# Batch 0's transform of a Fourier-and-MLP kernel: the last sums of phase 0 given to TensorE, with a new order of the opening

## The chip, the cores and the metric

The kernel runs on one core of a Trainium2 chip. The metric is device microseconds for one execution, the median of several runs. The engines are TensorE (PE, whose weight loads are listed as PEld), VectorE (DVE), ScalarE (ACT), GpSimd (POOL) and SyncE (SP), whose queue issues all the DMAs. Each engine takes its own instructions strictly in the order in which they are written, and waits for the others by semaphores.

## The reference

```python
batch, seq, dim = (8, 3008, 256)
X = np.fft.fft(x, axis=1)
X = np.fft.fft(X, axis=2)
attn_out = X.real.astype(np.float32)
...
x = attn_out.reshape(B * S, D)
h = x @ w_in          # 256 -> 2048
r = np.maximum(h, 0.0)
g = s * (r * r) + b
return (g @ w_out).astype(np.float32)   # 2048 -> 256
```

So the real part of a two-dimensional Fourier transform, for each of eight batches, goes through a two-layer network with a squared ReLU.

## The kernel before, in words

The transform along the 256 features is folded into w_in: `fold_w_in` multiplies the decoded w_in by cosine and sine tables (`feat_sb`) in four parts of 512 columns, and the results, split into a high and a low part, are the weights `wd_h` and `wd_l` of the first layer. The transform along the sequence stays. It uses symmetry: sequence rows are summed and subtracted (`load_rows`, line 502, and `load_pairs`, line 507), then the two halves of the features are summed and subtracted (`load_halves`, lines 515 and 516, the last level of sums), which gives the tile `cs` in `folded[0]`: eight leaves of 96 rows for each of two phases. Four rows of tile each lie apart and are put in place by ScalarE (`gather`, line 479). `transform(su, ph)` then combines leaves (`leaves_x`, `leaves_y`) and multiplies them with the table `dft_sb`; its helper `pair` does so for two leaves, with four matmuls of 96 columns at line 561: the cosine table on the sums of the feature halves, the sine table on their differences. The results go through DVE (lines 569 and 570) and ScalarE into the blocks `spec_h` and `spec_l`, high and low part of the spectrum. Feature 128 (the Nyquist feature) has a path of its own, `nyquist`, with many small POOL instructions (lines 349 to 369) and the matmuls of line 449.

A batch has 3 blocks of 502 columns, a block 16 steps. A step of the first layer is six matmuls (line 641) of weights and spectrum in high and low parts; DVE (lines 647, 650, 651) and ScalarE (652, 667, 673) make the activation and its high part `gh`, POOL or DVE the low part `gl` (line 676). A step of the second layer is twelve matmuls (line 696); in block 0's first four steps it is four plain fp32 matmuls instead (line 686). Everything in PSUM passes through two rings of four banks, `ab` and `po`; a bank can be written again only when its readers are done.

The order of all work is written out by hand as letters: `START` for batch 0 with all loads, then `BATCH` seven times. Each letter advances one generator in the dictionary `work` by one piece: X loads an x tile, N the Nyquist rows, r a piece of w_in, R of w_out, t a table, c the feature tables; x, d, g (phase 0) and y, Y (phase 1) are the sums on tiles, k and K the gathers; a, b, e decode w_in (A, B, E w_out; the addition at line 301 is POOL's), w folds it; n, m are the Nyquist path, s and u the transform of batch 0, phases 0 and 1; L, D, G, S are first layer, activation, low part and second layer of a step. All engines get their instructions in this order, so a letter's place sets its place in five queues at once.

Of the kernel before, what the change touches and what calls it, by code (L numbers as in the profile page):

```python
# [15 lines left out]
P = 128  # L16
# [4 lines left out]
R = 96  # L21
# [95 lines left out]
def _dft_tables():  # L117
# [45 lines left out]
    return np.ascontiguousarray(out.astype(np.float32))  # L163


def _turn_table():

    t = np.arange(P)
    t[T:] = 0
    a = np.pi * (2 * t + 1) / Q  # L170
    b = np.pi * (2 * t + 1) / H
    c = np.pi / 4 - b
    v = np.stack([np.tan(a), np.tan(b), np.tan(c), np.cos(c) / np.cos(b)], axis=1)
    return np.ascontiguousarray(np.concatenate([v, -v], axis=1).astype(np.float32))


def _feature_tables():

    l = np.arange(D)[:, None]
    d = np.arange(P)[None, :]  # L180
    c, s = _unit(2 * l * d, D)
    c[:, 0] *= 0.5

    s[:, 0] = np.where(l[:, 0] % 2 == 0, -1.0, 1.0)
    t = np.concatenate([c, -s], axis=1).astype(np.float32)
    return np.ascontiguousarray(t.reshape(2, P, 2 * P))
# [52 lines left out]
def kernel(ctx: ExitStack, tc: tile.TileContext, xq, xn, dft, turn, feat, w_in, w_out, s, b, out):  # L239
# [26 lines left out]
    feat_sb = const.tile([P, 2, 2 * P], F32, name="feat_sb")  # L266
    sb_s = const.tile([P, 1], F32, name="sb_s")
    sb_b = const.tile([P, 1], F32, name="sb_b")
    turn_sb = const.tile([P, 8], F32, name="turn_sb")
# [48 lines left out]
    def fold_w_in(f):  # L318

        at = slice(f * 512, (f + 1) * 512)  # L320
        pool, name = ((ps_ab, "ab"), (ps_o, "po"))[f in FOLDS_IN_SUMS]
        ps = [pool.tile([P, 512], F32, name=name) for _ in range(2)]
        for c in range(2):
            for kind in range(2):
                nc.tensor.matmul(  # L325
                    ps[kind], feat_sb[:, c, kind * P:(kind + 1) * P], halves[f, c], start=c == 0, stop=c == 1
                )
            yield
        row = rows[f][0:1]
        nc.scalar.copy(row, ps[1][0:1])  # L330
        split(wd_h[:, 1, at], wd_l[:, 1, at], ps[1], nc.vector)
        yield
        split(wd_h[:, 0, at], wd_l[:, 0, at], ps[0], nc.vector)
        yield
        nc.sync.dma_start(wny_dram[:, at], row)
        yield
        nc.sync.dma_start(wny[:, 4 * f:4 * f + 4], wny_dram[0, at].rearrange("(j p) -> p j", p=P))
        yield
# [127 lines left out]

    spec_tiles = {}
# [39 lines left out]
    def load_pairs(tiles, ph):  # L507
        for t in tiles_in_turn(tiles):
            (sub if ph else add)(t[:, 1 + 2 * ph], t[:, 0], t[:, 2])
            yield  # L510

    def load_halves(tiles, ph):
        for c, t in enumerate(tiles_in_turn(tiles)):
            t, v = t[:, 1 + 2 * ph], folded[0][:, ph, c + 2]
            add(v[:, :P], t[:, :P], t[:, P:])
            sub(v[:, P:], t[:, :P], t[:, P:])
            yield
# [5 lines left out]
    def gathers(ph):  # L523
        for c in range(NX):
            gather(folded[0], c, slice(ph, ph + 1))
            yield
# [24 lines left out]
    def transform(su, ph):  # L551
# [191 lines left out]
    def load_constants():  # L743
        nc.sync.dma_start(feat_sb, feat.rearrange("c p d -> p c d"))
# [99 lines left out]
    def second():  # L844
# [10 lines left out]
        "x": load_rows(tiles), "d": load_pairs(tiles, 0), "g": load_halves(tiles, 0), "k": gathers(0),  # L855
        "y": load_pairs(tiles, 1), "Y": load_halves(tiles, 1), "K": gathers(1),
# [74 lines left out]
```

## Time and profile before

| | us |
|---|---|
| median of 3 runs | 1592.61 |
| lowest and highest | 1591.66, 1593.21 |
| the profiled execution | 1592.15 |
| its span on the core | 1590.4 |
| PE busy | 1559.5 (98%) |
| ACT busy | 1268.6 (80%) |
| DVE busy | 1251.7 (79%) |
| POOL busy | 916.6 (58%) |

The span is the profiled execution without what lies around it, 1.75 us here. Times in rows are microseconds from the span's start. An engine's busy time is the sum over its instructions; PE's is modelled, since matmuls are pipelined, so that a row of several matmuls runs a little into the next. What ended an idle time stands in a row behind an arrow; it costs something only where the engine is the one that all others wait for.

### The profile page before, as it was taken

To read this page: it belongs to the slowest core of one execution; us is meant where nothing else is said; L and a number is where in the kernel's file an instruction comes from. 1 tells how busy PE (TensorE), PEld (TensorE's weight loads), DVE (VectorE), ACT (ScalarE), POOL (GpSimd) and SP (SyncE) were. 2 spreads that over 40 slices of the span, in tenths; PEclk is the share of its full clock that TensorE was granted. 3 is DMA by queue.
4 is the path that set the end of the run, shared out by engine and by line. 5 is a ranking of instruction groups with operands and counts; after the bars stand their busy time and mean duration, and the time that the engine had idled before them with its cause. 6 is when DMAs were issued, how large, how long until landed. Compare 5 with 4: busy or idle time off the path is not lost.

```text
span 1590.4 us, 21860 instructions
## 1 busy us (share of the span) xinstructions
PE 1559.5 (98%) x7494; PEld 1367.2 (86%) x7494; DVE 1251.7 (79%) x1912; ACT 1268.6 (80%) x1361; POOL 916.6 (58%) x541
## 2 busy tenths in 40 slices
PE   5899999999999999999999999999999999999998
PEld 2488898888888889888888888888888888988887
DVE  5888788699877998779886898868888699775563
ACT  4789787887787878878777887878788787787886
POOL 5455565555665556655565656555556555675554
PEclk8999999999999999999999999999999999999999
DMA  6402101021010100111001100102101020010000
GB/s 243 125 15 86 33 1 59 1 86 34 1 60 27 60 33 1 60 53 34 33 14 46 66 21 33 60 1 78 38 4 60 0 86 33 1 33 30 4 27 26
DMA packets 26070, 67.84 MB, mean 43 GB/s; under 512 B 5220, under 2 KB 10724, under 8 KB 25960
## 3 DMA queue, kind: packets, MB, share of 16 engines
q1 hardware_dynamic: 25960, 66.44, 12.5%
q8 instruction: 60, 0.98, 0.3%
q14 instruction: 50, 0.41, 0.1%
HBM read 41.70 MB, written 24.73 MB: 42 GB/s over the span
## 4 chain that ended last, share of the span: by engine, by line
PE 94%; DVE 2%; ACT 0%; issue 0%; POOL 0%; ACTq 0%; DVEq 0%; POOLq 0%
PE po L696 60%; PE ab L641 30%; PE ab L561 3%; PE po L686 1%; DVE uv L347 0%; DVE even L647 0%; DVE h L650 0%; DVE h L651 0%; PE ab L325 0%; DVE gl L676 0%; POOL gl L676 0%; DVE x L569 0%; ACT h L667 0%; ACT h L652 0%; DVE wd_l L263 0%
## 5 line engine op out<-in xcount | busy, mean ns | idle before, releaser
L676 POOL TENSOR_TENSOR gl<-h,gh 128x1004 fp32r<-128x1004 f32 x373 | 808.0, 2168 | 589.4 <-ACT gh L673 433.6
L652 ACT ACTIVATE h<-h 128x1004 f32<-128x1004 f32 x384 | 398.8, 1039 | 256.5 <-DVE h L651 238.8
L647 DVE SCALAR_TENSOR_TENSOR even<-ebc,wny,ab 128x502 f32<-128x502 f32 x384 | 281.4, 733 | 218.4 <-PE ab L641 209.1
L696 PE MATMUL po<-gh,wo_h 128*128 128x502 f32 (+1 forms) x1520 | 448.6, 377 | 0.0
L696 PE MATMUL po<-gh,wo_l 128*128 128x502 f32 (+1 forms) x1520 | 445.9, 375 | 0.0
L667 ACT ACTIVATE h<-h 128x1004 f32<-128x1004 f32 x380 | 395.6, 1041 | 12.0
L673 ACT CAST gh<-h 128x1004 fp32r<-128x1004 f32 x380 | 391.2, 1029 | 12.1
L696 PE MATMUL po<-gl,wo_h 128*128 128x502 f32 (+1 forms) x1520 | 384.6, 376 | 0.6 <-POOL gl L676 0.6
L696 PEld LDWEIGHTS po<-gl,wo_h 128*128 128x128 f32 x1520 | 286.6, 189 | 37.7 <-POOL gl L676 3.3
L696 PEld LDWEIGHTS po<-gh,wo_l 128*128 128x128 f32 x1520 | 287.1, 189 | 34.6
L696 PEld LDWEIGHTS po<-gh,wo_h 128*128 128x128 f32 x1520 | 284.3, 189 | 35.1 <-issue 1.0
L650 DVE TENSOR_TENSOR h<-even,ab 128x502 f32<-128x502 f32 x384 | 260.2, 678 | 55.8 <-POOL gl L676 3.2
L641 PE MATMUL ab<-spec_h,wd_h 128*128 128x502 f32 x768 | 292.5, 381 | 2.6 <-ACT spec_h L546 0.8
L641 PE MATMUL ab<-spec_l,wd_h 128*128 128x502 f32 x768 | 288.5, 376 | 0.3 <-POOL spec_l L549 0.3
L641 PE MATMUL ab<-spec_h,wd_l 128*128 128x502 f32 x768 | 287.1, 374 | 0.0
L651 DVE TENSOR_TENSOR h<-even,ab 128x502 f32<-128x502 f32 x384 | 257.7, 671 | 0.0
L641 PEld LDWEIGHTS ab<-spec_h,wd_h 128*128 128x128 f32 x768 | 144.7, 188 | 28.8 <-issue 4.6
L641 PEld LDWEIGHTS ab<-spec_l,wd_h 128*128 128x128 f32 x768 | 144.7, 188 | 18.4 <-issue 0.9
L641 PEld LDWEIGHTS ab<-spec_h,wd_l 128*128 128x128 f32 x768 | 145.0, 189 | 17.5
L713 DVE TENSOR_SCALAR o<-po,sb_s,bias 128x502 f32<-128x502 f32 x94 | 68.8, 794 | 29.0 <-PE po L696 29.0
L549 POOL TENSOR_TENSOR spec_l<-o,spec_h 128x368 fp32r<-128x368 f32 (+3 forms) x80 | 60.4, 777 | 30.4 <-ACT spec_h L546 29.8
L561 PEld LDWEIGHTS ab<-dft_sb,lf 96*128 96x128 f32 x384 | 47.9, 191 | 4.3 <-DVE even L647 1.8
(93 smaller groups left out, 772.0 us busy)
## 6 DMA issues: line engine op xcount, KB each, us to landing
out<-o SPq DMA_DIRECT2D x46, 502.0 KB
xt<-in_xq SPq DMA_DIRECT2D x44, 512.0 KB
raw<-in_w_in SPq DMA_DIRECT2D x8, 512.0 KB
ebc<-e_dram SPq DMA_DIRECT2D x16, 251.0 KB
cs<-in_xq SPq DMA_DIRECT2D x4, 512.0 KB
raw<-in_w_out SPq DMA_DIRECT2D x4, 512.0 KB
cs<-in_w_out SPq DMA_DIRECT2D x4, 512.0 KB
ebc<-e_dram SPq DMA_DIRECT2D x8, 126.0 KB
```

Source lines behind the costliest of these rows:

```text
L549: nc.gpsimd.tensor_sub(lo, src, hi.bitcast(F32))
L561: nc.tensor.matmul(ps[:, kind, i], src[:, i, kind * P:(kind + 1) * P], dft_sb[:R, ph, kind, leaf + i], start=True, stop=True,)
L641: nc.tensor.matmul(beside(ps[kind]), w[:, kind, fj], in_turn(m[:, kind]), start=i == 0, stop=i == 2)
L647: nc.vector.scalar_tensor_tensor(beside(even), in_turn(ebc), wny[:, j:j + 1], beside(ps[0]), op0=ALU.mult, op1=ALU.add)
L650: sub(h[:, 1], even, ps[1])
L651: add(h[:, 0], even, ps[1])
L652: nc.scalar.activation(h, h, AF.Relu)
L667: nc.scalar.activation(h, h, AF.Square)
L673: nc.scalar.copy(gh_halves, h)
L676: engine.tensor_sub(gl_halves, h, gh_halves.bitcast(F32))
L696: nc.tensor.matmul(beside(po[2 * pm + dh][:, :n]), l[:, j % 2, dh * P:(dh + 1) * P], in_turn(r[:, pm])[:, :n // 2], start=start and i in ( ...
L713: nc.vector.tensor_scalar(o[:, dh], po[2 * pm + dh][:, :NT], *args, ALU.mult, ALU.add)
```

## The change

The last level of sums of batch 0's phase 0 is left out of the loading: `load_pairs` writes the unsummed feature halves a and b straight into the place in `folded[0]`, `load_halves` does phase 1 alone, and the letter g is gone. For (batch 0, phase 0) `pair` multiplies a with the table [cos, sin] and b with a second one, [cos, -sin], into the same bank, 192 columns each. The second table comes in two pieces into buffers of the ring "gh", which the activations use later. The table argument that held the turns (`turn`) now holds phase 1's tables; the turns are eight more columns of the feature table, so their own DMA is gone. `START` has six letters fewer and another order throughout; `BATCH` is the same.

```diff
 START = (
-    "X N r X a x n r d b x y c d y X X X g Y a b e k g X w x r s K t k t x d Y d x g g r e w t k y d k x y r a g K "
+    "N X r c a r X a X n X x y X d Y b b x r e x d X d x k y a k d y x K s y w x k d t d R k Y r k t Y e w k s b Y "
...
+def _dft_tables():
+
+    t = _tables_of_both()[:, 0]
+    return np.ascontiguousarray(np.stack([t, np.stack([t[:, 0], -t[:, 1]], axis=1)], axis=1))
...
-    feat_sb = const.tile([P, 2, 2 * P], F32, name="feat_sb")
+    feat_sb = const.tile([P, 4 * P + 8], F32, name="feat_sb")
+    turn_sb = feat_sb[:, 4 * P:]
...
-    def load_pairs(tiles, ph):
+    def load_pairs(tiles):
+        for i, t in enumerate(tiles_in_turn(tiles)):
+            add(folded[0][:, 0, i + 2], t[:, 0], t[:, 2])
+            yield
+
+    def load_differences(tiles):
         for t in tiles_in_turn(tiles):
-            (sub if ph else add)(t[:, 1 + 2 * ph], t[:, 0], t[:, 2])
-            yield
...
+            sub(t[:, 3], t[:, 0], t[:, 2])
+            yield
+
+    def load_halves(tiles):
+        for i, t in enumerate(tiles_in_turn(tiles)):
+            v = folded[0][:, 1, i + 2]
+            add(v[:, :P], t[:, 3, :P], t[:, 3, P:])
+            sub(v[:, P:], t[:, 3, :P], t[:, 3, P:])
             yield
...
             ps = bank()[:, :4 * NL].rearrange("p (k i g) -> p k i g", k=2, i=2)
+            if (su, ph) == (0, 0):
+                for i in range(2):
+                    both_kinds = dft_sb[:R, 0, :, leaf + i], beside_b[leaf // 4][:R, :, leaf % 4 + i]
+                    for half, moving in enumerate(both_kinds):
+                        nc.tensor.matmul(
+                            ps[:, :, i], src[:, i, half * P:(half + 1) * P], moving, start=half == 0, stop=half == 1
+                        )
+                yield
+                return small.tile([P, 2, 4 * NL], F32, name="t", tag="tmp"), ps
...
         nc.sync.dma_start(t_ny, xn)
-        nc.sync.dma_start(turn_sb, turn)
...
-            nc.sync.dma_start(dft_sb[:, ph, :, leaves], dft[:, ph, :, leaves])
+            nc.sync.dma_start(dft_sb[:, ph, :, leaves], (dft[:, 0], dft_second)[ph][:, :, leaves])
+            if ph == 0:
+                beside_b.append(act.tile([P, 2, 4, NL], F32, name="dft_b", tag="gh"))
+                nc.sync.dma_start(beside_b[-1], dft[:, 1, :, leaves])
             yield
```

PE's queue from its first instruction, before: L325 is the fold of w_in, L449 the first Nyquist group, L561 the groups of `pair`.

```order
L325 MATMUL po<-bits,feat_sb 128x512 x4
L449 MATMUL ab<-dft_sb,room 16x384
L449 MATMUL ab<-dft_sb,room 16x8x24 x2
L449 MATMUL ab<-dft_sb,room 16x2x48 x4
L449 MATMUL ab<-dft_sb,room 16x96 x2
L449 MATMUL ab<-dft_sb,room 16x192
L449 MATMUL ab<-dft_sb,room 16x96 x2
L561 MATMUL ab<-dft_sb,cs 128x96 x4
L561 MATMUL ab<-dft_sb,lf 128x96 x4
```

PE's queue from its first instruction, now: L336 is the fold, L580 the new groups, L460 the Nyquist group.

```order
L336 MATMUL po<-bits,feat_sb 128x512 x4
L580 MATMUL ab<-dft_sb,cs 128x2x96
L580 MATMUL ab<-dft_b,cs 128x2x96
L580 MATMUL ab<-dft_sb,cs 128x2x96
L580 MATMUL ab<-dft_b,cs 128x2x96
L580 MATMUL ab<-dft_sb,lf 128x2x96
L580 MATMUL ab<-dft_b,lf 128x2x96
L580 MATMUL ab<-dft_sb,lf 128x2x96
L580 MATMUL ab<-dft_b,lf 128x2x96
L460 MATMUL ab<-dft_sb,room 16x384
```

The fold of the first 512 columns stays first; two groups of the transform, with the two tables in turn, now stand ahead of the Nyquist group.

SP's queue from the feature table on, before; in_xq are the x tiles, in_dft the tables.

```order
L744 DMA feat_sb<-in_feat 128x2x256
L740 DMA cs<-in_xq 128x1024 x2
L740 DMA xt<-in_xq 128x1024 x2
L760 DMA raw<-in_w_in 128x1024
L752 DMA dft_sb<-in_dft 128x2x384 x2
L760 DMA raw<-in_w_in 128x1024
L752 DMA dft_sb<-in_dft 128x1536
L760 DMA raw<-in_w_in 128x1024 x2
L335 DMA wny_dram<-raw 1x512
```

The same stretch of SP's queue now; ahead of it stand in_xn, one x tile and one piece of w_in.

```order
L769 DMA feat_sb<-in_feat 128x520
L788 DMA raw<-in_w_in 128x1024
L765 DMA cs<-in_xq 128x1024 x3
L765 DMA xt<-in_xq 128x1024
L788 DMA raw<-in_w_in 128x1024
L765 DMA xt<-in_xq 128x1024
L777 DMA dft_sb<-in_dft 128x2x384
L780 DMA dft_b<-in_dft 128x2x384
L801 DMA raw<-in_w_out 128x2x512
L788 DMA raw<-in_w_in 128x1024
L777 DMA dft_sb<-in_dft 128x2x384
L780 DMA dft_b<-in_dft 128x2x384
```

The feature table moved from the seventh place to the fourth, the third piece of w_in ahead of the last x tile, and the second table's pieces stand behind the first's.

ScalarE's queue up to the first use of the fold's result (L330), before; L293 and L295 decode w_in, L404 prepares the Nyquist rows, L479 gathers.

```order
L293 ACTIVATE bits<-raw 128x512
L295 ACTIVATE raw<-raw 128x512
L404 ACTIVATE room<-room 96x8x8 x5
L293 ACTIVATE bits<-raw 128x512
L295 ACTIVATE raw<-raw 128x512
L479 COPY cs<-cs 32x256 x5
L293 ACTIVATE bits<-raw 128x512
L295 ACTIVATE raw<-raw 128x512
L479 COPY cs<-cs 32x256
L330 COPY raw<-po 1x512
L262 CAST wd_h<-po 128x512 x2
```

The same stretch now.

```order
L304 ACTIVATE bits<-raw 128x512
L306 ACTIVATE raw<-raw 128x512
L304 ACTIVATE bits<-raw 128x512
L306 ACTIVATE raw<-raw 128x512
L415 ACTIVATE room<-room 96x8x8 x5
L491 COPY cs<-cs 32x256
L304 ACTIVATE bits<-raw 128x512
L306 ACTIVATE raw<-raw 128x512
L491 COPY cs<-cs 32x256 x6
L341 COPY raw<-po 1x512
L273 CAST wd_h<-po 128x512
L601 COPY t<-ab 128x2x96
```

Six gathers now stand behind the third decoding, and the transform's first copy (L601) stands between the two casts of the fold.

## Rows read from the trace of the kernel before

**Rows 1.** The page's part 1: busy time, share of the span, instructions of each engine.

```profile
PE 1559.5 (98%) x7494; PEld 1367.2 (86%) x7494; DVE 1251.7 (79%) x1912; ACT 1268.6 (80%) x1361; POOL 916.6 (58%) x541
```

**Rows 2.** PE's waits, 0 to 300 us: who waited for whom, total us, times, longest.

```profile
PE po L325 <- POOL bits L301: 8.2, 1, 8.2
PE ab L325 <- DVE wd_l L263: 2.2, 1, 2.2
PE ab L641 <- ACT spec_h L546: 0.8, 1, 0.8
```

**Rows 3.** From the chain that ended last: start us, us, what.

```profile
297.12 3.83 PE ab L641 x18
```

**Rows 4.** PE's timeline, 40 to 110 us: start, us, operation, shapes, [idle <-releaser].

```profile
45.91 0.48 PE L641 MATMUL ab<-spec_h,wd_h 128*128 128x502 f32 x1 [0.82 <-ACT spec_h L546]
...
50.50 3.47 PE L325 MATMUL ab<-bits,feat_sb 128*128 128x512 f32 x4 [2.15 <-DVE wd_l L263]
...
56.79 3.54 PE L686 MATMUL po<-g,whole 128*128 128x504 f32 x8
60.17 1.03 PE L561 MATMUL ab<-dft_sb,lf 96*128 96x96 f32 x8
...
80.44 0.59 PE L696 MATMUL po<-gh,wo_h 128*128 128x504 f32 x2
```

**Rows 5.** The timeline of all engines, 0 to 40 us; here PE's.

```profile
11.60 3.75 PE L325 MATMUL po<-bits,feat_sb 128*128 128x512 f32 x4 [11.60 <-DMA feat_sb<-in_feat]
...
23.55 3.78 PE L325 MATMUL po<-bits,feat_sb 128*128 128x512 f32 x4 [8.20 <-POOL bits L301]
...
31.46 1.13 PE L561 MATMUL ab<-dft_sb,cs 96*128 96x96 f32 x8
...
33.41 4.09 PE L449 MATMUL ab<-dft_sb,room 96*16 96x384 f32 x30
```

**Rows 6.** POOL's timeline: the addition of line 301, twice.

```profile
13.50 10.00 POOL L301 TENSOR_TENSOR bits<-bits,raw 128x512 int32<-128x512 int32 x1 [2.23 <-ACT cs L479]
...
27.94 1.28 POOL L301 TENSOR_TENSOR bits<-bits,raw 128x512 int32<-128x512 int32 x1
```

**Rows 7.** DVE's timeline, 8 to 30 us; left out are 25 rows without idle time.

```profile
13.49 0.28 DVE L516 TENSOR_TENSOR cs<-cs 128x128 f32<-128x128 f32 x1
13.69 0.68 DVE L504 TENSOR_TENSOR cs<-cs 128x512 f32<-128x512 f32 x1
...
21.95 0.41 DVE L298 TENSOR_SCALAR bits<-bits 128x512 int32<-128x512 int32 x1
28.51 1.29 DVE L263 TENSOR_TENSOR wd_l<-po,wd_h 128x512 fp32r<-128x512 f32 x2 [6.15 <-ACT wd_h L262]
```

**Rows 8.** Stretches: busy us (instructions) of five engines, clock, DMA share, GB/s.

```profile
11.60:15.40 3.80, 3.75 (x4) 1.14 (x4) 3.80 (x13) 1.59 (x4) 1.90 (x1) 1.00 1.03 412
...
31.40:45.90 14.50, 13.67 (x88) 9.49 (x86) 11.44 (x26) 9.99 (x30) 4.38 (x4) 1.00 0.47 134
48.40:50.50 2.10, 0.00 (x0) 0.00 (x0) 2.10 (x3) 2.10 (x5) 2.10 (x2) 0.91 0.82 172
50.50:53.30 2.80, 2.80 (x5) 1.25 (x5) 2.46 (x4) 1.18 (x3) 0.58 (x3) 0.50 0.75 247
```

**Rows 9.** DMA issues, 0 to 110 us: what, how many, KB each.

```profile
raw<-in_w_in SPq DMA_DIRECT2D x8, 512.0 KB
...
dft_sb<-in_dft SPq DMA_DIRECT2D x2, 384.0 KB
...
feat_sb<-in_feat SPq DMA_DIRECT2D x1, 256.0 KB
```

**Rows 10.** ScalarE's timeline, 8 to 30 us: a decoding and two gathers.

```profile
10.75 0.67 ACT L293 ACTIVATE bits<-raw 128x512 f32<-128x512 f32 x1 [0.61 <-DMA raw<-in_w_in]
...
12.66 0.81 ACT L479 COPY cs<-cs 32x256 f32<-32x256 f32 x2 [0.67 <-DVE cs L516]
```

**Rows 11.** Two of the stretches of 10 us; columns as in rows 8.

```profile
60.00:70.00 10.00, 9.21 (x38) 6.02 (x36) 9.70 (x16) 6.95 (x12) 6.01 (x6) 1.00 0.37 105
70.00:80.00 10.00, 9.91 (x31) 5.59 (x30) 7.42 (x11) 9.52 (x11) 5.58 (x12) 1.00 0.64 183
```

More of the change, by code (lines that the diff above doesn't have):

```diff
@@ L114, in _columns, with _tables_of_both @@
     return np.concatenate(ks)[order], np.concatenate(turned)[order]
-def _dft_tables():
+def _tables_of_both():
     t = np.arange(T)[:, None]
@@ L162, in _dft_tables, with _turns @@
                 rotated(4 + 2 * i, 5 + 2 * i, mq[i].reshape(1, NL), sg4, 376, _unit(half, H)[0])
-    return np.ascontiguousarray(out.astype(np.float32))
+    return out.astype(np.float32)
+def _dft_tables():
+    t = _tables_of_both()[:, 0]
+    return np.ascontiguousarray(np.stack([t, np.stack([t[:, 0], -t[:, 1]], axis=1)], axis=1))
 def _turn_table():
+    return np.ascontiguousarray(_tables_of_both()[:, 1])
+def _turns():
     t = np.arange(P)
@@ L173, in _turn_table @@
     v = np.stack([np.tan(a), np.tan(b), np.tan(c), np.cos(c) / np.cos(b)], axis=1)
-    return np.ascontiguousarray(np.concatenate([v, -v], axis=1).astype(np.float32))
+    return np.concatenate([v, -v], axis=1)
 def _feature_tables():
@@ L184, in _feature_tables @@
     s[:, 0] = np.where(l[:, 0] % 2 == 0, -1.0, 1.0)
-    t = np.concatenate([c, -s], axis=1).astype(np.float32)
-    return np.ascontiguousarray(t.reshape(2, P, 2 * P))
+    t = np.concatenate([c, -s], axis=1).reshape(2, P, 2 * P).transpose(1, 0, 2).reshape(P, 4 * P)
+    return np.ascontiguousarray(np.concatenate([t, _turns()], axis=1).astype(np.float32))
 def _rows():
@@ L238, with kernel @@
 @with_exitstack
-def kernel(ctx: ExitStack, tc: tile.TileContext, xq, xn, dft, turn, feat, w_in, w_out, s, b, out):
+def kernel(ctx: ExitStack, tc: tile.TileContext, xq, xn, dft, dft_second, feat, w_in, w_out, s, b, out):
     nc = tc.nc
@@ L263, in split @@
         lo_engine.tensor_sub(lo, src, hi.bitcast(F32))
-    feat_sb = const.tile([P, 2, 2 * P], F32, name="feat_sb")
+    feat_sb = const.tile([P, 4 * P + 8], F32, name="feat_sb")
+    turn_sb = feat_sb[:, 4 * P:]
     sb_s = const.tile([P, 1], F32, name="sb_s")
     sb_b = const.tile([P, 1], F32, name="sb_b")
-    turn_sb = const.tile([P, 8], F32, name="turn_sb")
     bias = const.tile([P, 2], F32, name="bias")
@@ L325, in fold_w_in @@
                 nc.tensor.matmul(
-                    ps[kind], feat_sb[:, c, kind * P:(kind + 1) * P], halves[f, c], start=c == 0, stop=c == 1
+                    ps[kind], feat_sb[:, (2 * c + kind) * P:(2 * c + kind + 1) * P], halves[f, c], start=c == 0, stop=c == 1
                 )
@@ L465, in nyquist @@
         yield
+    beside_b = []
     spec_tiles = {}
@@ L505, in load_rows @@
             yield
-    def load_pairs(tiles, ph):
+    def load_pairs(tiles):
[3 more added lines that the diff above has]
+    def load_differences(tiles):
         for t in tiles_in_turn(tiles):
-            (sub if ph else add)(t[:, 1 + 2 * ph], t[:, 0], t[:, 2])
+            sub(t[:, 3], t[:, 0], t[:, 2])
             yield
[L512 to L516, printed above, removed]
+    def load_halves(tiles):
[3 more added lines that the diff above has]
+            sub(v[:, P:], t[:, 3, :P], t[:, 3, P:])
             yield
@@ L523, in gathers @@
     def gathers(ph):
-        for c in range(NX):
-            gather(folded[0], c, slice(ph, ph + 1))
+        for i in range(NX):
+            gather(folded[0], i, slice(ph, ph + 1))
             yield
@@ L743, in load_constants @@
     def load_constants():
-        nc.sync.dma_start(feat_sb, feat.rearrange("c p d -> p c d"))
+        nc.sync.dma_start(feat_sb, feat)
         yield
@@ L854 @@
         "N": load_nyquist(), "X": load_x(), "c": load_constants(), "t": tables(),
-        "x": load_rows(tiles), "d": load_pairs(tiles, 0), "g": load_halves(tiles, 0), "k": gathers(0),
-        "y": load_pairs(tiles, 1), "Y": load_halves(tiles, 1), "K": gathers(1),
+        "x": load_rows(tiles), "d": load_pairs(tiles), "k": gathers(0),
+        "y": load_differences(tiles), "Y": load_halves(tiles), "K": gathers(1),
         "r": load_w_in(), "a": begin_w_in(), "b": go_on(in_progress), "e": go_on(in_progress), "w": fold_weights(),
```

16 rows, old and new, of the table START are left out of this document.

## The prediction

> **What bounds the kernel now.** I read the page first: TensorE (PE) is busy for 1559.5 us of a span of 1590.4 us, on one core [rows 1]. What PE does can be moved but hardly shortened, so what an order can win lies in the 31 us in which PE does nothing, and in stretches at its lower clock. The list of PE's waits came second: after the 11.6 us ahead of its first matmul, one wait of 8.2 us for the second half of the first weight fold and one of 2.2 us for a PSUM bank; the rest are under 1 us each [rows 2]. All of these lie in the first 51 us; later, 18 matmuls of L641 take 3.83 us without a gap [rows 3], 1.28 us for one step of the first layer. So I compare the time at which PE reaches two points: F0, the first step of the first layer (45.91 us now), and S0, the first second-layer step of three products (80.44 us) [rows 4]. What PE has done by then is the same list of work before and after.
>
> **Why F0 is late now.** PE's queue begins with the fold of w_in's first 512 columns: two matmuls at 11.60 us, two at 23.55 us, and all else behind them [rows 5]. The second pair waits for one POOL addition, issued at 13.50 us, which took 10.00 us; the same addition takes 1.28 us at 27.94 us [rows 6]. Meanwhile VectorE (DVE) ran from 13.49 to 22.36 us, 29 instructions, each starting before the one ahead had ended and nearly all with two inputs in SBUF; the POOL addition ended 1.1 us after the last of them [rows 6, 7]. I read this as POOL shut out until DVE pauses. The Trainium skill ("SBUF — State Buffer", section "Who interferes with whom") says that a DVE instruction with two SBUF inputs contends with a GpSimd instruction that reads SBUF, and that whichever issues second blocks until the first finishes. By that rule as worded POOL would have had its turn after one DVE instruction; the row shows a wait for 29 of them, and the row decides. By the rule rival (a) would be void and the sum the same.
>
> **Part 1: a new first transform.** Twelve DVE instructions go, the six sums and six differences of the two feature halves in phase 0 (L515, L516): 0.28 us each, their starts 0.2 us apart [rows 7], 2.4 us of DVE. PE makes up for it: each of the four pair() groups of batch 0's phase 0 has four matmuls of 192 columns in place of four of 96. A group of 96 columns takes 1.03 us [rows 4]. A plain second-layer step has four matmuls of 502 or 504 columns and takes 3.4 us to the next group's start (56.79 to 60.17 us) [rows 4], 0.85 us for each, so 192 columns take 0.32 us and a group 1.3 us. That is +0.3 us for a group, between nothing (if the weight loads set the pace still) and +1.0 us; it is counted in Part 3. The second table costs two DMAs of 384 KB each.
>
> **Part 2: when the transform can start.** Its inputs set it, so I go by the DMA queue. It moves 412 GB/s from 11.60 us on [rows 8], so 512 KB take 1.28 us and 384 KB 0.95 us [rows 9]. In the kernel before, 2436 KB had been asked for up to and with the feature table, whose landing let PE start at 11.60 us [rows 5]; in the new order the same sum is reached with x tile 1. I put tile 1 at 11.6 us and count on: tiles 2, 3, 4 at 12.9, 14.2, 15.4 us, w_in piece 2 at 16.7, tile 5 at 18.0, the first phase-0 table at 19.0, its second form at 19.9 us. The last input is ScalarE's: from 16.7 us it decodes w_in piece 2 (two instructions of 0.67 us as at 10.75 us) and then gathers six times at 0.4 us [rows 10], which ends at 20.4 us. DVE's work on tile 5 is three instructions of 0.68 us at most [rows 7], from 18.0 us, and is earlier. **So pair(0) stops waiting at 20.4 us, where it starts at 31.46 us now** [rows 5]. The fold must be over by then. Its first half needs w_in piece 0 as now and the features, now ahead of piece 1, so not later than 11.6 us. Its second half needs the POOL addition, ready about when x tile 1 lands; DVE has 0.7 us of work on that tile and then waits for tile 2, so POOL finds a pause and is done by about 13.5 us. At the pace of the first half, 3.75 us [rows 5], both end by 19.1 us.
>
> **Part 3: from pair(0) to F0.** PE's list: four groups of phase 0 at 1.3 us, the second Nyquist group 4.1 us (30 records), the first 3.3 us (24 records at the same pace) [rows 5], the second fold 3.4 us, two groups of phase 1 at 1.0 us: 18.0 us. Waits: the second group of phase 1 takes the PSUM bank that the second fold's result leaves by way of ScalarE and DVE; laid out with the durations above, 1.3 us, between none and 4 us. The clock: PE has gaps until 20.4 us, and in the kernel before 2.1 us without matmuls (48.4 to 50.5 us) were followed by 2.8 us at a granted clock of 0.50 [rows 8], the 1.2 GHz level. There two fold matmuls took 2.8 us where 1.7 us do; I take 1.7 us of loss, between none and 4 us. Half of pair(0) can run ahead of 20.4 us: -0.6 us. Sum: 20.4 + 18.0 + 1.3 + 1.7 - 0.6 = 40.8 us, against 45.91: **-5.1 us**, between -9 and +2 us if all bounds fell together.
>
> **Part 4: from F0 to S0.** 34.5 us now. Work: eight first-layer steps at 1.28, the third fold 3.4, four plain steps at 3.4, one group at 1.0: 28.2 us. So 6.3 us are lost now, to late input at F0, to the bank wait ahead of 50.50 us and to the half clock behind it [rows 2, 4, 8]. In the new order the whole third fold follows two steps of the first layer, so PE has 1.3 us more to do ahead of the bank that it waits for. I lay DVE's and ScalarE's queues out and find them just in time, with under 0.5 us to spare at the third fold and at the first and third plain steps; ends: none of the 6.3 us lost, or all. I take half: **-3.1 us**.
>
> **Part 5: behind S0.** The steps are the same. DVE is busy for 9.70 of 10 us from 60 us and ScalarE for 9.52 from 70 us [rows 11]; PE is now 8 us further ahead, and DVE's own idle time, 22.4 to 28.5 us [rows 7], is filled. I allow **+0.6 us**, between -1 and +5 us. The sum is -5.1 - 3.1 + 0.6 = -7.6 us: 1592.15 - 7.6 = 1584.55 us for the profiled execution, whose time stands 0.46 us under the median of the three runs. I say **1585.0 us**.
>
> **Rivals.**
> (a) The shut-out moves. POOL's 21 small instructions for the second Nyquist group and two decodings (L301) stand where DVE works on tiles 2 to 5; if POOL loses again, the second fold waits in place of the first. For: the 10.00 us. Against: from the first wd_l on, DVE reads PSUM and one SBUF input, and no row shows POOL held up by that. Part 3's gain is gone, Parts 4 and 5 stay: 1592.6 - 2.5 = 1590.1 us; 1587.5 us if half of it goes.
> (b) The gain is given back behind S0, because ScalarE and DVE, not PE, set the pace of the first steps. For: the shares in [rows 11]. Against: PE's waits there are short in the kernel before [rows 2]. All but 2 us goes: 1590.6 us.
> (c) Slower: the half clock stays. If PE, fed in pieces by tables, POOL and banks, is granted 0.50 all through pair(0) to F0, 18.0 us of matmuls take up to 36.0 us and F0 comes at 56 us, 10 us later than now; with Parts 4 and 5, 1600 us. It decides from where some 15 us more than I allow run at 0.50, since each costs half a microsecond. For: the fold at 23.55 us, after a wait of 8.2 us, ran as slowly as the one at 11.60 us [rows 5]. Against: 13.67 of 14.5 us from 31.4 us were busy at 1.00 with the same groups [rows 8]. The Trainium skill ("TensorE: Matmul & The Clock Gate", section "HAM oscillation — how this bites in real kernels") tells of a kernel that falls to half clock at each wait for data; here the rows show single falls only.
> (d) The change does not do what it says: the removed sums were off the path, and pair(0) waits for what stands behind them, the fold at half clock or the table's second form. That costs up to 3 us of Part 3: 1588 us.
>
> **How the numbers follow.** Forecast 0.70; (a) 0.11, (b) 0.07, (c) 0.06, (d) 0.06. The forecast's own range is 1579.5 us (Part 4's loss gone and 2 us more of Part 3) to 1590.5 us (no gain in Part 4, half of Part 3's); (d) and (a) lie in it, (b) at its end. So 1579.5 to 1590.5 leaves out (c) and some of both tails. A difference under 0.2%, 3.2 us, can hardly be told from none here. Faster by more: nearly all of the forecast, half of (a), most of (d): 0.80. Within: the rest of these and (b): 0.13. Slower: (c) and a little of (b): 0.07.
>
> **What would show it.** Pair(0) starts at 19 to 22 us; the first fold's POOL additions take under 3 us each; F0 comes at 38.5 to 43 us and S0 at 69 to 76 us; PE has no wait of over 1 us after that; the granted clock is 0.50 for one stretch of 3 to 7 us around pair(0). I am wrong if a POOL row of L301's kind takes 5 us or more, if the table's second form lands after 22 us, or if S0 comes early and the end does not.

## The result: 1578.3 us, a ratio of 0.991

| | before | after |
|---|---|---|
| median, us | 1592.4 | 1578.32 |
| lowest and highest | 1591.66, 1593.21 | 1577.40, 1579.28 |
| the profiled execution | 1592.15 | 1577.40 |
| its span | 1590.4 | 1575.6 |
| F0, first step of the first layer | 45.91 | 39.87 |
| S0, first second-layer step of three products | 80.44 | 67.97 |
| F0 to S0 | 34.5 | 28.1 |
| S0 to the end of the span | 1509.92 | 1507.65 |

The ratio is 0.9911, with an interval from 0.9894 to 0.9929. The span is 14.8 us shorter: 6.0 us are won ahead of F0, 6.4 between F0 and S0, 2.3 behind S0. I had said 5.1, 3.1 and a loss of 0.6. The result lies 1.2 us below my range.

The distances are read from one execution, the profiled one; eight executions of the new program, four here and four in e5, took 1575.00 to 1579.28 us.

The page's part 1 of the new kernel, to compare with [rows 1]: DVE has its twelve instructions less, and PE is busy for 2.3 us less, though each new group takes longer.

```profile
PE 1557.2 (99%) x7494; PEld 1370.4 (87%) x7494; DVE 1250.0 (79%) x1900; ACT 1268.3 (80%) x1361; POOL 910.3 (58%) x541
```

PE's waits in the first 300 us (who waited for whom, total us, times, longest), where [rows 2] had 8.2 us for POOL, 2.2 us for a bank and a tail of short ones:

```profile
PE po L336 <- POOL bits L312: 10.2, 1, 10.2
PE ab L580 <- ACT cs L491: 2.4, 1, 2.4
PE ab L580 <- DMA dft_b<-in_dft: 0.3, 1, 0.3
```

These three are all: ahead of the first matmul, and at the first group of the transform. After 18.8 us PE waits for nothing. PE's timeline, to compare with [rows 4, 5] (L336 is the fold, L580 a new group, L460 Nyquist, L667 the first layer, L722 the second):

```profile
10.19 5.30 PE L336 MATMUL po<-bits,feat_sb 128*128 128x512 f32 x8 [10.19 <-POOL bits L312]
17.92 0.59 PE L580 MATMUL ab<-dft_sb,cs 96*128 96x192 f32 x2 [2.44 <-ACT cs L491]
18.80 0.59 PE L580 MATMUL ab<-dft_b,cs 96*128 96x192 f32 x2 [0.29 <-DMA dft_b<-in_dft]
...
22.34 5.42 PE L460 MATMUL ab<-dft_sb,room 96*16 96x384 f32 x24
...
32.54 0.49 PE L580 MATMUL ab<-dft_sb,lf 96*128 96x192 f32 x2
...
33.84 1.03 PE L587 MATMUL ab<-dft_sb,cs 96*128 96x96 f32 x8
...
39.87 0.48 PE L667 MATMUL ab<-spec_h,wd_h 128*128 128x502 f32 x1
...
67.97 0.59 PE L722 MATMUL po<-gh,wo_h 128*128 128x504 f32 x2
```

The fold runs through, both halves in 5.30 us, where a wait of 8.2 us lay between them. The first matmul starts 1.4 us earlier, and behind it PE waits for 2.7 us ahead of F0 in place of 8.2. Stretches (us, then busy us and instructions of PE, PEld, DVE, ACT, POOL, then the granted clock, the DMA share and GB/s) show the rest: half clock behind the wait (0.50 from 20.3 to 27.0 us), and from F0 to S0 a PE that is busy all the time.

```profile
15.50:17.90 2.40, 0.00 (x0) 0.00 (x0) 2.38 (x7) 2.32 (x6) 2.17 (x7) 1.00 1.06 383
...
20.70:27.60 6.90, 6.90 (x30) 4.32 (x28) 6.06 (x15) 4.07 (x9) 1.38 (x2) 0.54 1.05 390
...
39.90:68.00 28.10, 28.10 (x98) 17.55 (x98) 25.29 (x46) 25.45 (x38) 13.48 (x18) 1.00 0.38 123
```

The kernel before had half clock ahead of F0 too, behind its wait of 8.2 us, and the second half of its first fold ran in it:

```profile
23.50:29.60 6.10, 6.05 (x10) 2.02 (x11) 1.09 (x2) 2.12 (x5) 4.94 (x22) 0.50 0.19 53
```

The clock column cannot be trusted at the very start: it shows 1.00 for the new kernel's first fold, whose eight matmul records take 5.30 us, while those of the second fold take 3.60 us at 1.00 (from 29.10 us).

### The profile page after: what moved, and what is told of

Its sections match the earlier page's. It is cut to its first block, busy times and chain, and to the rows that moved or that the text cites. A ratio compares the mean times of both kernels' runs of the same rounds, so it can differ in the third digit from the quotient of the medians.

```text
span 1575.6 us, 21849 instructions
## 1 busy us (share of the span) xinstructions
PE 1557.2 (99%) x7494; PEld 1370.4 (87%) x7494; DVE 1250.0 (79%) x1900; ACT 1268.3 (80%) x1361; POOL 910.3 (58%) x541
## 4 chain that ended last, share of the span: by engine, by line
PE 98%; DMA 1%; SPq 0%; ACTq 0%; issue 0%; ACT 0%
PE po L722 61%; PE ab L667 31%; PE ab L587 3%; PE po L712 1%; PE ab L336 1%; DMA dft_b<-in_dft 1%; PE ab L460 1%; PE ab L580 0%; DMA raw<-in_w_in 0%; ACTq L947 0%; SPq L769 0%; SPq L788 0%; SPq L765 0%; SPq L755 0%; ACT o L737 0%
## 5 line engine op out<-in xcount | busy, mean ns | idle before, releaser
L722 PE MATMUL po<-gh,wo_h 128*128 128x502 f32 (+1 forms) x1520 | 448.2, 376 | 0.0
L722 PE MATMUL po<-gh,wo_l 128*128 128x502 f32 (+1 forms) x1520 | 445.9, 375 | 0.0
L722 PE MATMUL po<-gl,wo_h 128*128 128x502 f32 (+1 forms) x1520 | 384.4, 375 | 0.0
L722 PEld LDWEIGHTS po<-gl,wo_h 128*128 128x128 f32 x1520 | 286.8, 189 | 36.5 <-POOL gl L702 2.3
L722 PEld LDWEIGHTS po<-gh,wo_l 128*128 128x128 f32 x1520 | 287.1, 189 | 34.6
L722 PEld LDWEIGHTS po<-gh,wo_h 128*128 128x128 f32 x1520 | 284.4, 189 | 34.6 <-issue 0.5
L676 DVE TENSOR_TENSOR h<-even,ab 128x502 f32<-128x502 f32 x384 | 260.2, 678 | 55.5 <-POOL gl L702 3.6
L667 PE MATMUL ab<-spec_h,wd_h 128*128 128x502 f32 x768 | 291.6, 380 | 0.1
L667 PE MATMUL ab<-spec_l,wd_h 128*128 128x502 f32 x768 | 288.3, 375 | 0.0
L667 PE MATMUL ab<-spec_h,wd_l 128*128 128x502 f32 x768 | 287.1, 374 | 0.0
L667 PEld LDWEIGHTS ab<-spec_h,wd_h 128*128 128x128 f32 x768 | 144.6, 188 | 23.2 <-issue 3.6
L667 PEld LDWEIGHTS ab<-spec_h,wd_l 128*128 128x128 f32 x768 | 145.0, 189 | 17.5
L667 PEld LDWEIGHTS ab<-spec_l,wd_h 128*128 128x128 f32 x768 | 144.7, 188 | 17.5 <-issue 0.7
L739 DVE TENSOR_SCALAR o<-po,sb_s,bias 128x502 f32<-128x502 f32 x94 | 68.8, 794 | 30.1 <-PE po L722 30.1
L501 DVE TENSOR_TENSOR xt<-xt 128x512 f32<-128x512 f32 x42 | 50.6, 1204 | 0.1
```

Of the source, the lines that this page charges most:

```text
L501: add(t[:, 0::2], t[:, 0::2], t[:, 1::2])
L667: nc.tensor.matmul(beside(ps[kind]), w[:, kind, fj], in_turn(m[:, kind]), start=i == 0, stop=i == 2)
L676: sub(h[:, 1], even, ps[1])
L722: nc.tensor.matmul(beside(po[2 * pm + dh][:, :n]), l[:, j % 2, dh * P:(dh + 1) * P], in_turn(r[:, pm])[:, :n // 2], start=start and i in ( ...
L739: nc.vector.tensor_scalar(o[:, dh], po[2 * pm + dh][:, :NT], *args, ALU.mult, ALU.add)
```

## The experiments

Twelve kernels. F0 and the two distances are read from each kernel's profiled execution; S53 is the first matmul of the 54th second-layer step of three products, S0 that of the first. The median and the profiled execution can lie apart: the latter took 1584.04 us in e2, 3.5 us under the median, and 1587.21 us in e8, 3.5 us over it.

| kernel | median us | ratio to before | F0 | F0 to S0 | S0 to S53 |
|---|---|---|---|---|---|
| before | 1592.4 | | 45.91 | 34.5 | 214.0 |
| after | 1578.32 | 0.9911 | 39.87 | 28.1 | 211.3 |
| e1 order alone | 1579.49 | 0.9916 [0.9902, 0.9931] | 42.10 | 28.1 | 211.3 |
| e2 transform alone | 1587.53 | 0.9963 [0.9952, 0.9975] | 38.11 | 34.8 | 213.7 |
| e3 addition on DVE | 1587.33 | 0.9967 [0.9954, 0.9980] | 39.34 | 35.5 | 213.7 |
| e6 addition in four | 1593.35 | 1.0006 [0.9996, 1.0015] | 44.20 | 35.4 | 214.0 |
| e7 third fold split | 1576.70 | 0.9901 [0.9881, 0.9921] | 40.04 | 28.1 | 211.7 |
| e8 second fold late | 1583.75 | 0.9950 [0.9934, 0.9966] | 47.67 | 30.1 | 211.3 |
| e11 second fold early | 1591.24 | 0.9992 [0.9982, 1.0002] | 46.71 | 32.2 | 213.7 |
| e9 tail as before | 1578.57 | 0.9913 [0.9893, 0.9932] | 39.63 | 28.1 | 213.4 |
| e4 four idle matmuls | 1576.04 | 0.9897 [0.9880, 0.9914] | 37.25 | 28.1 | 211.3 |
| e5 same queues | 1576.65 | 0.9899 [0.9884, 0.9914] | 37.40 | 28.1 | 211.3 |
| e10 tables first | 1576.26 | 0.9899 [0.9882, 0.9915] | 37.92 | 28.1 | 211.3 |
| e12 tables first, b | 1574.80 | 0.9890 [0.9873, 0.9906] | 37.18 | 28.1 | 211.3 |

The last two columns hold the main finding. Except where an experiment moves that very stretch of the order (e7, e8, e11, e9), F0 to S0 takes 28.1 us and S0 to S53 211.3 us with the new order, some 35 and 214 us with the old one, however early PE arrives. PE has the same matmuls to do between F0 and S0 in every kernel.

### The two halves of the change: e1 and e2

```diff
-            add(folded[0][:, 0, i + 2], t[:, 0], t[:, 2])
+            add(t[:, 1], t[:, 0], t[:, 2])
...
 START: after each "d" a "g" (sums and differences of the halves, phase 0); one table, old pair()
```

> The new order with the old transform: the last level of sums of phase 0 is back on DVE (twelve instructions, each right behind its tile's first-phase sum), there is no second table, and the groups have 96 columns again. Theory O (the order made the gain): DVE has 2.4 us more before the gathers, so pair(0) starts at 19.5 to 21.5 us instead of 17.9, PE has 1.3 us less to do, F0 comes at 40 to 42 us, S0 at 68 to 70 us and the time is 1577 to 1581 us. Theory T (leaving out the sums made it): F0 at 43 us or later and 1586 to 1592 us.

```diff
 START of before without its six "g"; new pair(), second table
+        nc.sync.dma_start(turn_sb, turn)
```

> The order of the kernel before, without its six letters for the removed sums, with the new transform, its second table and the turns by a DMA of their own as before. Theory O: the POOL addition of the first fold still takes 7 us or more, F0 comes at 43 to 46 us and the time is 1588 to 1594 us. Theory T: F0 at 41 us or earlier, 1578 to 1583 us.

(e1 keeps the turns in the feature table, e2 has their own DMA again.) The order alone gives 13.1 us by the medians, where the whole change gives 14.1 us and, in a second series of the new kernel (e5), 16.3 us. In e1 pair(0) waits for the gathers a second time, until 21.32 us, and F0 comes 2.2 us later than with the new transform. Part of this is clock: the granted clock was 0.50 from 19.1 to 29.2 us in e1. The transform alone, in the old order, brings F0 to 38.11 us in its profiled execution, earlier than the whole change does: POOL's addition takes 1.61 us, although DVE does not pause, and the clock does not fall between the fold and F0. Then it loses it again: the waits between F0 and S0 are those of [rows 2], with a stretch at 0.50 behind them as in [rows 8]. PE's waits of e2, 0 to 75 us:

```profile
...
PE ab L336 <- DVE wd_l L274: 2.1, 1, 2.1
...
PE ab L667 <- ACT spec_h L563: 0.8, 1, 0.8
...
PE ab L667 <- DVE t L596: 0.6, 1, 0.6
```

Both halves free POOL, so their gains ahead of F0 do not add up; the gains behind F0 belong to the order.

### POOL's addition of 10.00 us: e3 and e6

```diff
-        nc.gpsimd.tensor_add(bits, bits, low)
+            nc.vector.tensor_tensor(bits, bits, low, op=ALU.bitwise_or)   # second piece of w_in only
```

> The kernel before, but the one addition of the first fold that took 10.00 us on POOL (w_in piece 1) is done by DVE as a bitwise or, at the same place in the order. Theory S (that wait alone made F0 late): the fold's second half starts at 17 to 18.5 us instead of 23.55, F0 comes 4 to 6 us earlier, and if the loss between F0 and S0 follows from lateness too, the time is 1580 to 1585 us; if that loss belongs to the order, 1586 to 1589 us. Rival: the transform's inputs or POOL's small Nyquist instructions are late anyway, F0 at 44 us or later, 1590 to 1593 us.

```diff
+        n = 512 // pieces                # pieces is 4 for the second piece of w_in, else 1
+        for k in range(pieces):
+            at = slice(k * n, (k + 1) * n)
+            nc.gpsimd.tensor_add(bits[:, at], bits[:, at], low[:, at])
```

> The kernel before, with the POOL addition of w_in piece 1 cut into four instructions of 128 columns. If POOL is shut out until DVE pauses (my reading of the row of 10.00 us), the first of the four already takes 8 us or more, all four end after 22.4 us and the time stays at 1591 to 1594 us. If POOL gets a turn for each instruction at the end of a DVE instruction, as the skill's page has it, the four end by 17 us and F0 comes 4 to 6 us earlier. If POOL advances a little at each DVE instruction, each of the four takes about a quarter, 2 to 2.5 us, and the end is the same as for one.

In e6 the four quarters together took 10.42 us. By tile, they are (x4: shortest, median and longest in ns; first and last start in us):

```profile
L304 POOL TENSOR_TENSOR bits<-bits,raw x4: 452/452/9181, 12.9 to 22.8; 128x128 int32<-128x128 int32 x4
```

One quarter, the first, took 9.18 us, the other three 0.45 us each behind DVE's last instruction. So the addition was not slowed all along; POOL did not get past the first quarter until DVE stopped at 21.7 us. (F0 comes 1.7 us earlier here than before: the clock stood at 1.00 from 26.7 us to F0, where before it stood at 0.50 until 29.6 us. Behind F0 it stood at 0.50 from 46.9 to 53.6 us.) e3 takes the addition off POOL: the second half of the fold comes at 18.3 us in place of 23.55 and F0 6.6 us earlier. But now another POOL instruction is held up, one of 96x8 elements that takes 0.20 us elsewhere, and in the new kernel none is (POOL's timelines, first e3, then after):

```profile
13.21 0.73 POOL L353 TENSOR_TENSOR room<-room 96x8 f32<-96x8 f32 x1
13.90 8.63 POOL L352 TENSOR_TENSOR room<-room,turn_sb 96x8 f32<-96x8 f32 x1
22.61 0.20 POOL L353 TENSOR_TENSOR room<-room 96x8 f32<-96x8 f32 x1
```

```profile
10.56 1.61 POOL L312 TENSOR_TENSOR bits<-bits,raw 128x512 int32<-128x512 int32 x1 [0.42 <-ACT room L415]
...
16.45 0.26 POOL L361 TENSOR_TENSOR room<-room 96x8 f32<-96x8 f32 x1
16.68 0.74 POOL L360 TENSOR_TENSOR room<-room,feat_sb 96x8 f32<-96x8 f32 x1
17.50 0.26 POOL L361 TENSOR_TENSOR room<-room 96x8 f32<-96x8 f32 x1
```

From 12.70 to 20.00 us in the new kernel DVE is busy for 6.89 us of 7.30, and POOL still gets its 21 instructions through, each ending within one or two of DVE's. The Trainium skill ("SBUF — State Buffer", section "Who interferes with whom") has the second to issue block until the first finishes. The new kernel's rows agree with that, 0.20 to 0.74 us each; the 8.63, 9.18 and 10.00 us do not. My reading of [rows 6, 7], that POOL is shut out until DVE pauses, holds for these three and not in general. Nor are these two the only forms. In e2, beside a DVE that ran on, POOL got in behind several of DVE's instructions:

```profile
13.96 2.40 POOL L410 COPY room<-room 96x16 f32<-96x16 f32 x1
16.32 0.65 POOL L360 TENSOR_TENSOR room<-room,turn_sb 96x8 f32<-96x8 f32 x1
17.05 1.53 POOL L361 TENSOR_TENSOR room<-room 96x8 f32<-96x8 f32 x1
```

What decides how long POOL waits I have not found.

### The 6.4 us between F0 and S0: e7, e8 and e11

```diff
-... m L w b A e a D E D w w E w ...
+... m w w w L b A e a D E D E w ...
```

(The three "w" are two small DMAs of the second fold and the third fold's first two matmuls, now ahead of the second step.)

> The new kernel with one edit in PE's queue: the third fold is cut in two, its first two matmuls between the first and the second step of the first layer (as in the kernel before), the other two where all four were. No other queue changes. It asks what took away the 6.3 us that the kernel before loses between F0 and S0 (34.5 us against 28.1 us in the new one). Theory 1, the bank wait came from the second fold standing just ahead of F0, so that its result had not left the banks: nothing waits here, only one more change between fp32 and fp32r matmuls; F0 to S0 takes 28.1 to 28.9 us. Theory 2, that of the prediction (the third fold kept whole behind two steps gives PE 1.3 us more to do ahead of the bank): the wait and the half clock behind it come back, 30 to 34.5 us. Theory 3, the order of DVE and ScalarE did it: 28.1 to 28.9 us, as by theory 1.

```diff
-... y i A e a s Y r s K w Y b w K u s u c w w s B B e u u u a s m L m L w ...
+... y i A e a s Y r s K Y b K u s u c s B B e u u u a s m w w w w L m L w ...
```

> The new kernel with the whole second fold (its four matmuls and the copies and differences of its result on ScalarE and DVE) moved from ahead of the last group of phase 0 to directly ahead of F0, about where the kernel before has it. The third fold stays whole behind two steps. Theory 1 (the second fold's place is what costs): the third fold or a step near it waits for DVE's wd_l, 1 us or more, and the clock may fall behind it; F0 to S0 takes 29.5 to 34.5 us. Theory 2 (the third fold whole behind two steps is what avoids the wait): no wait of 1 us, 28.1 to 28.5 us. Theory 3 (the order of DVE's and ScalarE's other work): at most 29 us.

```diff
 START of before:
-... e u s s b u u s b w u B u e s w w w e w r a R A L ...
+... e w w u w w s s b u u s b u B u e s e w r a R A L ...
```

> The kernel before with the second fold (four matmuls, its copies on ScalarE and its two differences on DVE) moved ahead of the second group of phase 0's second half, where the new kernel has it; all else as before. Moving it late in the new kernel brought a wait for wd_l of 1.23 us and 30.1 us from F0 to S0 in place of 28.1. Theory 1 (the fold's place makes the bank wait of 2.15 us and the half clock behind it, together 3.5 to 4 us): the wait ahead of the third fold is under 0.5 us, F0 to S0 takes 30 to 31.5 us in place of 34.5, the rest of the loss (late spec blocks at F0 and three short waits later) stays. Theory 2 (in the old order DVE and ScalarE are late with everything ahead of the third fold): another wait of about the same size takes its place, 33 to 34.5 us.

e7 settles one thing: with the third fold cut in two around the second step, F0 to S0 is 28.1 us to the hundredth. My own reason in Part 4, that the fold kept whole gives PE more to do ahead of the bank, is wrong. e8 and e11 move the second fold, each the other way. PE's waits in e8 (17 to 70 us; left out are the two ahead of the first groups) and in e11 (30 to 70 us):

```profile
...
PE ab L667 <- DVE wd_l L274: 1.2, 1, 1.2
...
```

```profile
PE ab L641 <- ACT spec_h L546: 2.9, 1, 2.9
PE ab L641 <- DVE t L570: 0.5, 1, 0.5
PE ab L641 <- DVE wd_l L263: 0.2, 1, 0.2
PE ab L561 <- DVE wd_l L263: 0.2, 1, 0.2
```

With the fold late, its result does not leave the banks in time: PE waits 1.23 us for wd_l and F0 to S0 grows by 2.0 us. With the fold early in the old order, the wait of 2.15 us ahead of the third fold is gone and F0 to S0 shrinks by 2.3 us, but F0 itself waits 2.86 us for spec_h in place of 0.82 us. ScalarE was idle for 3.13 us ahead of that cast; on DVE, the fold's differences now stand ahead of the spectrum's sums (wd_l at 41.97 us, the sums from 43.51 us). S0 comes at 78.94 us, 1.5 us earlier. The distance of 32.2 us lies between the ranges of both theories, and it holds a loss of its own, half clock behind the wait at F0:

```profile
46.70:51.40 4.70, 4.69 (x8) 2.80 (x9) 3.77 (x5) 4.16 (x9) 4.66 (x5) 0.50 0.48 160
```

So the second fold's place wins 2.3 of the 6.4 us in this run, and would win more if the wait at F0 did not bring half clock; a clean share cannot be read from it. That the rest comes from the order of ScalarE and DVE around F0, and from the clock behind the waits, is argued from the names in the waits (spec_h, spec_l, t, wd_l) and from the stretches; no run took these apart.

### The 2.3 us behind S0: e9

```diff
 START up to the fifth S as after, then what is left of each letter in the order of before:
-S f D B L e D G u S L l l S w E D w B f R D l G L G G S D ...
+f D w B S S G D u L D L S L E e D B E w G R A G S f D u B l ...
```

> The new kernel's order up to S0, and from there on the letters that are left in the order in which the kernel before has them. It asks why the time from S0 to the 637th second-layer matmul is 211.3 us in every kernel with the new order and 213.7 to 214.0 us in every one with the old, though PE has the same matmuls to do. Theory 1 (the order behind S0 alone, with late inputs near four steps): 213.5 to 214.2 us, PE idle four times for 1.2 to 1.6 us together, and a total of 1580 to 1581.5 us. Theory 2 (DVE and ScalarE are further ahead when S0 is reached, by the head of the order): 211.3 to 212 us and 1577.5 to 1579 us. The prediction's own Part 5 had +0.6 us here for a PE that is further ahead.

PE's waits of e9, 68 to 300 us; the new kernel has none there:

```profile
PE ab L667 <- DVE h L677: 0.7, 2, 0.4
PE po L722 <- POOL gl L702: 0.6, 1, 0.6
```

S0 to S53 is 213.4 us, with PE at S0 as early as in the new kernel. The medians do not show this: 1578.57 us of two executions (1577.28 and 1579.85) lies beside the new kernel's 1578.32 us and under the 1580 us that I had expected, since both programs vary by more than 2 us from one execution to the next. The distance itself hardly varies: it is 211.33 to 211.35 us in seven of the kernels with the new order. The kernel before has the same rows from 80 to 300 us, `PE ab L641 <- DVE h L651: 0.6, 2, 0.4` and `PE po L696 <- POOL gl L676: 0.6, 1, 0.6`. So the gain behind S0 is the order's there, and PE's being ahead costs nothing that can be seen. The named waits are 1.3 us of the 2.1 us by which e9 stands over the new kernel; the rest lies in gaps too short for the list of waits.

### The clock, and what pair(0) waits for: e5, e4, e10 and e12

```diff
-... L m L w b A e a D E D w w E w ...
+... L m w L w b A e a D E D w E w ...
```

> The changed kernel with one letter moved: the first half of the third fold stands between the first and the second step of the first layer, its second half stays, as in the kernel before. Theory P (placing the whole third fold behind two steps took away the loss between F0 and S0): PE waits 1.5 to 3 us for a bank again, the clock may fall behind it, S0 comes 1.5 to 5 us later and the time is 1580 to 1583 us. Rival L (that loss came from DVE and ScalarE being late, by the first fold and their clashes): PE waits under 0.7 us more and the time is 1577.5 to 1579 us.

The letter that moved stood for one of the fold's small DMAs, and every engine's queue stayed as it was. So nothing of this expectation was tested (e7 did that); e5 is a second series of the new kernel. Its profiled execution had no stretch at half clock and F0 at 37.40 us, where the first had 6.8 us at 0.50 and F0 at 39.87 us. The same program thus varies by 2.5 us at F0 with the clock alone, and its eight times go from 1575.00 to 1579.28 us.

```diff
+            if (su, ph, leaf) == (0, 0, 0):
+                beside_it_all = ps_o.tile([P, 512], F32, name="po")
+                for _ in range(4):
+                    nc.tensor.matmul(beside_it_all, feat_sb[:, :P], feat_sb[:, :4 * P], start=True, stop=True)
```

> The changed kernel with four more fp32 matmuls of 512 columns, whose result nobody reads, between the first fold and pair(0), where PE waits from 15.5 to 18.8 us. Theory C (the half clock from 20.7 to 27.6 us costs what it takes beyond full clock): the granted clock stays at 1.00, pair(0) ends within 0.5 us of now, the Nyquist group takes 3 us instead of 5.4, F0 comes 2.5 to 3.4 us earlier and the time is 1574.5 to 1576 us. Rival: the groups wait for DVE or the tables anyway, F0 within 0.8 us of 39.9 and the time 1577.5 to 1579 us; or the fill delays pair(0) and the time grows by up to 1 us.

```diff
 two of the idle matmuls, and in START
-... Y b b x r e x d X d x k y a k d ... k d t d R k Y r k t Y e w k s b ...
+... Y b b x e x d X d x k y k d ... k d t r d R k Y r k t Y e w k s a b ...
```

> The new kernel with the load of w_in's third piece moved behind the transform's first two tables, its decoding behind the six gathers, and two matmuls of 512 columns without use ahead of pair(0) (they cover half of PE's wait). Theory (x tiles, tables and gathers stand in one DMA queue at 1.28 us for 512 KB, so that pair(0) gets its inputs one piece earlier): pair(0) starts at 17.3 to 17.8 us in place of 18.8, F0 at 35.8 to 36.6 us without a stretch of half clock (37.25 us with four idle matmuls and the old loads), total 1574.3 to 1575.5 us. Rival: the third piece, decoded later, makes the second fold wait for POOL, or the first fold's copies wait for the decoding on ScalarE: the gain is gone, 1576 us or more.

```diff
 as e10, but
-... y x K s y w x k d t r d R k Y r k t Y e w k s a b Y w s w r ...
+... y x K y w x k d t r d s R k Y r k t Y e w k s Y w s w a b r ...
```

> As the kernel with the tables first (w_in's third piece loaded behind the first two tables, two matmuls without use ahead of pair(0)), but the third piece is decoded behind the casts of the first fold, and the sums for the second group stand behind x tile 5's on DVE. There pair(0) started at 18.40 us and the third group waited 1.38 us for DVE. Theory (DVE's queue, not the loads, set both): pair(0) at 17.2 to 18.0 us with no wait at the third group, F0 at 36.2 to 37.0 us, total 1574.3 to 1575.5 us. Rival: the second fold now waits for the third piece's POOL addition, F0 at 37.5 us or later, 1575.8 us or more.

With four idle matmuls in the gap the clock does not fall between the fold and F0; pair(0) then follows at 18.82 us. e10 gains nothing over that: its pair(0) starts at 18.40 us and the third group waits 1.38 us for DVE, so DVE's queue, not the loads alone, set the start. e12 mends that queue. PE's timeline of e12:

```profile
10.15 5.57 PE L336 MATMUL po<-bits,feat_sb 128*128 128x512 f32 x8 [10.15 <-POOL bits L312]
15.56 1.88 PE L579 MATMUL po<-feat_sb 128*128 128x512 f32 x4
17.28 0.49 PE L584 MATMUL ab<-dft_sb,cs 96*128 96x192 f32 x2
...
24.17 0.59 PE L584 MATMUL ab<-dft_sb,lf 96*128 96x192 f32 x2 [0.61 <-DVE lf L379]
```

Pair(0) starts at 17.28 us and F0 at 37.18 us, a little later than I had said, since three short waits came up (0.6, 0.5 and 0.3 us). Its four times, 1574.68 to 1574.89 us, lie below all eight of the new kernel's program, but by only 0.1 us below the lowest of these, which had no half clock. So what it wins over the new kernel is for the most part the clock.

The other side of the clock showed in e8 unasked. Its stretches:

```profile
17.70:19.20 1.50, 1.15 (x5) 0.73 (x5) 1.50 (x8) 1.41 (x5) 1.34 (x6) 0.92 1.07 401
19.20:43.10 23.90, 23.80 (x87) 18.16 (x87) 15.95 (x38) 13.63 (x36) 8.20 (x10) 0.50 0.65 227
43.10:47.60 4.50, 4.50 (x22) 2.45 (x20) 0.00 (x0) 0.00 (x0) 0.00 (x0) 1.00 0.00 0
```

The clock fell to the 1.2 GHz level behind the same wait as in the new kernel, but stayed there for 23.9 us of groups and Nyquist matmuls without a gap. F0 came at 47.67 us, 7.8 us later than in the new kernel, though PE had the same matmuls to do. This was the longest of e8's three executions (1583.04, 1583.75 and 1587.21 us); the others were not profiled. It is rival (c), in a kernel one move away.

## Why the prediction was wrong

**What bounds the kernel, and where the gain lies**: right as to what, wrong as to where. PE's idle time fell from 30.9 to 18.4 us and its busy time by 2.3 us, with half clock counted as busy. But I wrote that all of PE's waits lie in the first 51 us; the waits behind S0 shown at e9 lie later, and Part 5 has no term for them.

**Part 1**: right. A group of four matmuls of 192 columns takes 1.30 us (32.54 to 33.84 us); I had 1.3.

**Part 2**: the mechanism was right, the anchor late. I let x tile 1 land at 11.6 us, where the same number of bytes had landed before. DVE's and ScalarE's timelines of the new kernel show tile 2 and w_in's third piece, which I had at 12.9 and 16.7 us:

```profile
11.52 1.20 DVE L516 TENSOR_TENSOR cs<-cs 128x512 f32<-128x512 f32 x1 [0.50 <-DMA cs<-in_xq]
```

```profile
15.38 0.67 ACT L304 ACTIVATE bits<-raw 128x512 f32<-128x512 f32 x1 [4.04 <-DMA raw<-in_w_in]
...
16.63 2.52 ACT L491 COPY cs<-cs 32x256 f32<-32x256 f32 x6
```

The whole queue runs 1.3 us earlier, and the six gathers end at 19.15 us in place of 20.4: pair(0) is past its last input 1.3 us earlier. It started at 17.92 us, outside the 19 to 22 us that I had named as a sign. The anchor varies by itself: in e6, with the same loads as in the kernel before, the feature table let PE start at 10.95 us in place of 11.60.

**Part 3**: F0 at 39.87 us for 40.8, in the interval named. The bank wait of 1.3 us did not come; the half clock did, over 6.8 us, and cost 2.5 us by e5, where I took 1.7. The bounds of this part were added up too narrowly: by its own terms they come to -9.3 and +2.7 us, not -9 and +2.

**Part 4** is the first step that failed, a term mis-sized. I said that half of the 6.3 us goes; all of it went, and S0 came at 67.97 us, ahead of the 69 to 76 us that I had named. I had found DVE and ScalarE "just in time, with under 0.5 us to spare", and took the middle between two ends. But there the layout itself said zero: being in time by little is still in time, and e1, e4, e5, e7, e9, e10 and e12 are in time in the same way with F0 anywhere from 37.18 to 42.10 us. Its mechanism failed too (e7).

**Part 5** is the second, and there the sign was wrong. I priced PE's lead as a risk of 0.6 us from the busy shares [rows 11], and said that the steps are the same. They are, but not in the same order; the kernel before loses 1.4 us in listed waits behind S0, which I had passed over as short, and the new order loses none (e9). I put a gain there at 1 us at most, and 2.3 us were won. This step carried the result out of the range: my lower end took in all of Part 4's loss and 2 us more of Part 3, but left Part 5 at +0.6 us.

**Rivals.** (a) did not happen; the shut-out disappeared instead of moving, and e3 shows that it can move, to an instruction that nobody waits for. (b) fell with Part 5. (c) happened for one stretch only, and the profiled execution of e8 shows how near it was. (d) happened in its smallest form: pair(0) waited 0.29 us for the second table. The removed sums were on the path: with the old transform in the new order pair(0)'s last wait ends at 21.32 us in place of 18.80.

The sum, by the steps as measured: 6.0, 6.4 and 2.3 us make 14.7; I had 5.1, 3.1 and -0.6. Of the error of 7.2 us in the profiled execution, 0.9 are Parts 2 and 3, 3.3 Part 4, 2.9 Part 5.

## What to carry to other kernels

Where the whole order is new, list every wait of the bounding engine in the kernel before, the short ones far behind the opening too: each is something an order can win, and a lead over the other engines is no cost by itself. Where a layout of the queues comes out just in time, take it at its word and keep the loss for the range. And a short wait on TensorE can cost more in clock than in waiting (in e8, 1.8 us of waits and 23.9 us at half clock behind them); in e4, filling it with idle matmuls kept the clock up, and its four times lay within 1.0 us.

## What the hardware did that I had not expected

The granted clock can fall behind a short wait or not, and the length of the wait does not tell which: it fell behind one of 2.44 us in the new kernel and one of 0.98 us in e7, and did not behind one of 1.91 us in e5, the same program as the new kernel, nor behind one of 1.25 us in e2. Once low it stayed at 0.50 for 6.8 us in one kernel and for 23.9 us in another, with PE busy 23.80 us of them. The Trainium skill ("TensorE: Matmul & The Clock Gate", section "HAM oscillation — how this bites in real kernels") tells of falls at each wait for data; the long stretch of e8 has no wait in it, so that here it was not waiting that kept the clock down.

POOL beside a busy DVE can get its turn within one or two of DVE's instructions (in the new kernel 0.20 to 0.74 us for 96x8 elements, 1.28 to 1.61 us for 128x512), or behind several of them (1.53 and 2.40 us in e2), or not until DVE stops (8.63, 9.18 and 10.00 us). The first and the last occur in one trace (e3: 0.73 us at 13.21 us, 8.63 us at 13.90 us).
